# q and k transposed by the DMA crossbar instead of TensorE, in cosine attention followed by a gated feed-forward

## Chip, core and metric

One core of a Trainium2 chip. The metric is the device time of one launch in microseconds (us), the median of several executions. The engines go by short names: PE is TensorE, ACT is ScalarE, DVE is VectorE, POOL is GpSimd, SP is SyncE. Each has its own instruction stream; they meet at semaphores. PSUM is the memory that PE writes, in 8 banks.

## What is computed

Attention with q and k normalized to length 1 over 8 batches of 12 heads, 448 tokens and 64 features a head, then a multiplicative feed-forward on the 3584 tokens:

```python
q_n = q / (np.linalg.norm(q, axis=-1, keepdims=True) + 1e-06)
k_n = k / (np.linalg.norm(k, axis=-1, keepdims=True) + 1e-06)
scores = np.matmul(q_n, k_n.transpose(0, 1, 3, 2)) / tau          # tau = 0.1
scores = scores - np.max(scores, axis=-1, keepdims=True)
attn = np.exp(scores)
attn = attn / (np.sum(attn, axis=-1, keepdims=True) + 1e-09)
attn_out = np.matmul(attn, v)
x = attn_out.transpose(0, 2, 1, 3).reshape(3584, 768)
a = x @ w1                      # 768 x 1024
b = x @ w2
out = (a * b @ w3) @ w_out      # 1024 x 1024, then 1024 x 768
```

## The kernel before

The 96 heads are treated as 48 pairs of two heads; three pairs make a group that is loaded together. A pair goes through these steps:

1. q, k and v are loaded as bf16 (POOL issues the loads), with 112 tokens on the partitions and 4 tokens of each head along the row.
2. POOL squares q and k, DVE sums, ACT takes the root, and POOL scales (`prep_scale`): the result is `nrm`, bf16. A pair's q and k take 1024 columns of it on 112 partitions.
3. PE transposes each 112x128 block of `nrm` (two heads of 64 features side by side), 8 blocks a pair, into one PSUM bank, and DVE copies the bank to `qkT` in SBUF.
4. PE computes the scores of 112 keys (a chunk) against 448 queries, ACT takes exp of them, PE multiplies by v (`av`), which has a column of ones for the sum, and DVE divides (`osd`).
5. PE transposes `osd` back (`trback`), and DVE copies it to `xT`, the input of the feed-forward. The feed-forward of a batch (`a_group`, `b_group`, `out_group`) needs its six pairs. w3 @ w_out is multiplied out once.

```python
    def prep_scale(g, i, t, eng):
        if g not in nrms:
            nrms[g] = nrm_pool.tile([P, GP, 2, NJ, 2, D], BF16, tag="nrm", name="nrm")
        eng.tensor_mul(
            nrms[g][:, i, t].rearrange("p j h d -> p h j d"),
            raw_of(g, t, i),
            rns[g][:, t, 2 * i:2 * i + 2].to_broadcast([P, 2, NJ, D]))
    ...
    def tr(pp):
        g, i = divmod(pp, GP)
        n = nrms[g]
        ps = half(f"tr{pp}")
        for t in range(2):
            for j in range(NJ):
                nc.tensor.transpose(
                    ps[:, 1 - t, j * P:(j + 1) * P],
                    n[:, i, t, j].rearrange("p h d -> p (h d)"),
                    ident[:P, :P])
        qks[pp] = head_pool.tile([128, 2, S], BF16, tag="qkT", name="qkT")
        pst[pp] = ps

    def tr_copy(pp):
        nc.vector.tensor_copy(qks[pp], pst.pop(pp)[:, :, :S])

    def scores(name, chunks):
        for n, (pp, c) in enumerate(chunks):
            if c == 0:
                exps[pp] = exp_pool.tile([P, NJ, 2, S], BF16, tag="exp", name="expT")
            b = plan.bank[name][2 * n]
            sc = scs[pp, c] = ps_all[:, b:b + 2]
            for hh in range(2):
                kq = qks[pp][64 * hh:64 * hh + 64].rearrange("p t s -> p (t s)")
                nc.tensor.matmul(
                    sc[:, hh, :S], kq[:, c * P:c * P + 128], kq[:, S:],
                    start=True, stop=True)
    ...
    def av(pp, hh):
        g, i = divmod(pp, GP)
        vt = v_tiles[g % NV]
        ps = full(f"av{pp}.{hh}")[:, :NJ * (D + 1)].rearrange("p (m d) -> p m d", m=NJ)
        for m, q0 in enumerate(QT):
            for c in range(NJ):
                nc.tensor.matmul(
                    ps[:, m, :],
                    exps[pp][:, c, hh, q0:q0 + 128],
                    vt[:, 2 * i + hh, c, :D + 1],
                    start=(c == 0), stop=(c == NJ - 1))
        if hh == 0:
            osds[pp] = head_pool.tile([128, NJ, 2, D], BF16, tag="osd", name="osd")
    ...
    def mm_group(pairs, o):
        for i, (l, r) in enumerate(pairs):
            nc.tensor.matmul(o, l, r, start=(i == 0), stop=(i == len(pairs) - 1))
    ...
    def out_copy(bb, ch, cols, eng):
        ...
        elif cols.stop == DM:
            store(bb, ch, osbs.pop((bb, ch)), slice(None), (nc.sync,))
```

In the profile L291 is `prep_scale`, L310 the transposes in `tr`, L318 `tr_copy`, L328 the scores, L342 `av`, L364 and L371 the transposes back and their copy, and L377 all matmuls of the feed-forward.

The order in which each engine gets its instructions is not that of the text. A small planner (`Plan`) holds a list of steps, each with the engine or engines it may run on, an assumed duration in us, a rank, the steps it comes after and the buffers it takes and holds. It places the steps one by one, each as early as its engine, its inputs and its buffers allow; of those that could start about then, the lowest rank goes first. Attention has low ranks and the feed-forward high ones, so that feed-forward groups fill what attention leaves free. The result is one fixed order for each engine. The steps of the transposes and the scores:

```python
    plan = Plan(
        rings=dict(raw=3, vraw=2, vt=NV, sq=6, nrm=3, qkT=2, osd=2,
                   exp=3, xT=2, a_sb=KO2, big=1, out_sb=3), ...)
    ...
        add(f"sc{nb}", [("PE", 0.205 + 0.187 * len(ch))], ch[0][0] + 0.25 * ch[0][1] - 1,
            lambda e, nb=nb, ch=ch: scores(f"sc{nb}", ch),
            [f"ev{p}" for p in ps] + ([f"sc{nb - 1}"] if nb else []),
            [("exp", ("exp", p)) for p, c in ch if c == 0], [("qkT", p) for p in ps],
            banks=[tuple(slots)])
    ...
    for p in range(NP):
        g, i = divmod(p, GP)
        b, blk = divmod(p, NPAIR)
        last = p > 0
        add(f"tr{p}", [("PE", 0.4)], p - 1.2, lambda e, p=p: tr(p),
            [f"scale{p}.0", f"scale{p}.1", "ident"] + ([f"tr{p - 1}"] if last else []),
            [("qkT", ("qkT", p))], [("nrm", g)],
            slack=0.3 if g > 2 else 0.0, banks=SHORT)
        add(f"ev{p}", [("DVE", 0.54)], p - 1.1, lambda e, p=p: tr_copy(p), [f"tr{p}"],
            reads=[(f"tr{p}", None)])
```

Of the kernel before, what the change touches and what calls it, by code (L numbers as in the profile page):

```python
# [9 lines left out]
BF16 = mybir.dt.bfloat16  # L10
# [9 lines left out]
class Plan:  # L20
# [24 lines left out]
    def add(self, name, on, rank, emit, after=(), takes=(), holds=(), reads=(), kb=0, later=None,  # L45
            until=None, slack=0.0, port=False, lead=None, banks=()):
        if name in self.homes:
            on = [x for x in on if x[0] in self.homes[name]]
        self.steps[name] = dict(on=on, rank=rank, emit=emit, after=list(after), later=later,
                                takes=list(takes), kb=kb, until=until, slack=slack, port=port, lead=lead or {},  # L50
                                banks=banks)
        for user, part in reads:
            self.reads.setdefault(user, []).append((name, part))
        for key in holds:
            self.holders.setdefault(key, []).append(name)
# [45 lines left out]
    def order(self):  # L101
# [11 lines left out]
        out = []  # L113
        while ready:
# [17 lines left out]
            if st["port"] and eng in self.port:  # L132
                self.port[eng] = t + cost
            if st["kb"]:
                ring = max(ring, t + cost + self.DMA_FIRST) + st["kb"] / self.RATE
                self.end[n], self.where[n] = ring + self.DMA_LAST, "DMA"
                self.lanes.append(self.end[n])
# [17 lines left out]
def kernel(  # L155
# [28 lines left out]
    NFIRST = 6  # L184
    VROW = 80
    QT = (0, 128, 256, S - 128)

# [100 lines left out]
    def prep_scale(g, i, t, eng):  # L288
        if g not in nrms:
            nrms[g] = nrm_pool.tile([P, GP, 2, NJ, 2, D], BF16, tag="nrm", name="nrm")  # L290
        eng.tensor_mul(  # L291
            nrms[g][:, i, t].rearrange("p j h d -> p h j d"),
            raw_of(g, t, i),
            rns[g][:, t, 2 * i:2 * i + 2].to_broadcast([P, 2, NJ, D]))
# [9 lines left out]
# [4 lines that stand above are left out]
        for t in range(2):  # L308
            for j in range(NJ):
                nc.tensor.transpose(  # L310
                    ps[:, 1 - t, j * P:(j + 1) * P],
                    n[:, i, t, j].rearrange("p h d -> p (h d)"),
                    ident[:P, :P])
        qks[pp] = head_pool.tile([128, 2, S], BF16, tag="qkT", name="qkT")
        pst[pp] = ps

    def tr_copy(pp):
        nc.vector.tensor_copy(qks[pp], pst.pop(pp)[:, :, :S])  # L318
# [17 lines left out]
    def av(pp, hh):  # L336
# [10 lines left out]
        if hh == 0:  # L347
            osds[pp] = head_pool.tile([128, NJ, 2, D], BF16, tag="osd", name="osd")
        pav[pp, hh] = ps
# [8 lines left out]
    def trback(pp):  # L358
# [4 lines left out]
        for m, q0 in enumerate(QT):  # L363
            nc.tensor.transpose(  # L364
                ps[:, 0, q0:q0 + 128],
                osds[pp][:, m].rearrange("p h d -> p (h d)"), ident)
        pst["b", pp] = ps

    def tb_copy(pp):
# [82 lines left out]
    def out_copy(bb, ch, cols, eng):  # L452
# [4 lines left out]
        if at_end(bb, ch):  # L457
            store(bb, ch, osbs[bb, ch], cols, (nc.sync, nc.scalar) if cols.start else (nc.sync,))
        elif cols.stop == DM:
            store(bb, ch, osbs.pop((bb, ch)), slice(None), (nc.sync,))  # L460

# [22 lines left out]
    for eng, names in (  # L484
# [6 lines left out]
    plan = Plan(  # L491
        rings=dict(raw=3, vraw=2, vt=NV, sq=6, nrm=3, qkT=2, osd=2,
                   exp=3, xT=2, a_sb=KO2, big=1, out_sb=3),
        begin=dict(PE=1.0, ACT=3.0, DVE=1.2, POOL=1.3), homes=homes)
    add = plan.add
# [134 lines left out]
    for p in range(NP):  # L630
        g, i = divmod(p, GP)
        b, blk = divmod(p, NPAIR)
        last = p > 0
        add(f"tr{p}", [("PE", 0.4)], p - 1.2, lambda e, p=p: tr(p),
            [f"scale{p}.0", f"scale{p}.1", "ident"] + ([f"tr{p - 1}"] if last else []),
            [("qkT", ("qkT", p))], [("nrm", g)],
            slack=0.3 if g > 2 else 0.0, banks=SHORT)
        add(f"ev{p}", [("DVE", 0.54)], p - 1.1, lambda e, p=p: tr_copy(p), [f"tr{p}"],
            reads=[(f"tr{p}", None)])
        for h in range(2):  # L640
# [5 lines left out]
                lambda e, p=p, h=h: av_norm(p, h), [f"av{p}.{h}"], reads=[(f"av{p}.{h}", None)])  # L646
        add(f"tb{p}", [("PE", 0.235)], p + 1, lambda e, p=p: trback(p),
            [f"an{p}.0", f"an{p}.1"] + ([f"tb{p - 1}"] if last else []),
            [] if blk else [("xT", ("xT", b))], [("osd", p)], banks=SHORT)
        add(f"xt{p}", [("DVE", 0.31)], p - 0.2, lambda e, p=p: tb_copy(p), [f"tb{p}"],  # L650
            reads=[(f"tb{p}", None)])

# [29 lines left out]
    for b in range(B):  # L682
# [20 lines left out]
        for ch in (range(0, 3) if b % 2 == 0 else range(3, 7)):  # L703
            for cols in out_cols(bb, ch):
# [8 lines left out]
                     [("out_sb", ("out_sb", bb, ch))] if cols.start == 0 else [], [("big", bb)],  # L713
                     holds2=[("out_sb", bb, ch)] if cols.stop == DM else [],
                     lead={f"b{b}.{KO2 - 1}.c": 1.1, f"b{b}.{KO2 - 2}.c": 0.9})
    for n in range(60):
        add(f"warm{n}", [("PE", 0.78 if n < 4 else 0.39)], 10000 + n, lambda e, n=n: warm(n),
            banks=PM, later=f"warm{n - 1}" if n else None, until=6.5)
# [39 lines left out]
```

## Time and profile before

| | |
|---|---|
| time, median of 3 | 391.69 us (391.43 to 392.08) |
| span of the profiled execution | 390.0 us |
| granted PE clock | 0.999 of full speed |
| HBM read, written | 46.66 MB, 11.01 MB |
| PE transposes of q and k (L310) | 384, 212 ns each |
| DVE copies to qkT (L318) | 48, 615 ns each |
| DMAs issued by SP | 1 load and the output stores, 2.0 to 3.1 us from issue to landing |

The page gives each engine's busy time and its share of the span, then the span cut into 40 slices of 9.75 us with one digit a slice (9 is 90% busy or more), then the chain of work that ended last, followed back from the last instruction. The answers on waits list who waited for whom, with the total, the count and the longest; those on the timeline list runs of instructions with start and length. Durations of matmuls overlap, because they are pipelined: what one costs in a run is the distance from one start to the next.

### The profile page before, as it was taken

Reading aid. Unit: us, or ns where it says so; the run is one execution under the profiler, and the core shown is the slowest. Engines: PE = TensorE matmul, PEld = TensorE weight load, DVE = VectorE, ACT = ScalarE, POOL = GpSimd, SP = SyncE. Lnnn points to the kernel's source line nnn. Section 1 sums busy time; section 2 is a strip of 40 time slices with the busy share of each in tenths; the row PEclk is TensorE's granted clock in tenths of the full one; section 3 lists DMA queues with packets and bytes.
Section 4 is the critical chain, followed back from the end, with each engine's and each line's share of the span. In section 5 each row is a group of like instructions: output and inputs, shape, how many; then the busy total and the mean of one; then the engine's idle time right before and its main releaser. Section 6 shows DMA issues by size and latency. Waiting matters only on the chain.

```text
span 390.0 us, 9618 instructions
## 1 busy us (share of the span) xinstructions
PE 379.0 (97%) x3998; PEld 227.7 (58%) x3998; DVE 218.6 (56%) x500; ACT 242.0 (62%) x396; POOL 244.0 (63%) x258
## 2 busy tenths in 40 slices
PE   7789999999999999999999999999999999999995
PEld 3477666556565665556565565565656565565553
DVE  5899865587575844868477665553534444341210
ACT  5868865847756866747747776647466666652222
POOL 8687999999999989999999978361610000000000
PEclk9999999999999999999999999999999999999999
DMA  8999999637585467564738166202100121004005
GB/s 144 200 203 200 210 209 195 81 37 115 117 108 70 79 111 129 67 81 91 122 42 108 43 124 105 37 2 82 42 0 2 43 82 43 2 0 123 0 11 153
DMA packets 43707, 35.18 MB, mean 90 GB/s; under 512 B 3984, under 2 KB 37648, under 8 KB 43664
## 3 DMA queue, kind: packets, MB, share of 16 engines
q0 software_dynamic: 38384, 23.11, 43.2%
q1 hardware_dynamic: 4784, 11.07, 9.7%
q8 instruction: 31, 0.51, 0.5%
q10 hardware_dynamic: 496, 0.40, 0.3%
q14 instruction: 12, 0.10, 0.1%
HBM read 46.66 MB, written 11.01 MB: 148 GB/s over the span
## 4 chain that ended last, share of the span: by engine, by line
PE 91%; DMA 5%; DVE 2%; issue 1%; POOL 0%; DVEq 0%; POOLq 0%
PE ps L377 62%; PE ps L342 11%; PE ps L328 10%; PE ps L310 4%; DMA wo_sb<-in_moe_w_out_dram 4%; PE ps L364 3%; DMA w_sb<-in_moe_w_dram 2%; DVE nrm L291 1%; POOL raw L225 0%; DVE ss L263 0%; PE ps L390 0%; DVE qkT L318 0%; DVE osd L355 0%; DVE rn L286 0%; DVE w_sb L385 0%
## 5 line engine op out<-in xcount | busy, mean ns | idle before, releaser
L333 ACT ACTIVATE expT<-ps 112x896 bf16<-112x896 f32 x192 | 166.2, 920 | 34.1 <-PE ps L328 33.2
L377 PE MATMUL ps<-xT,w_sb 128*128 128x448 bf16 x768 | 161.3, 353 | 0.0
L377 PEld LDWEIGHTS <-w_sb 128*128 128x128 bf16 x768 | 69.2, 98 | 65.7 <-issue 12.6
L291 POOL TENSOR_TENSOR nrm<-raw,rn 112x512 bf16<-112x512 bf16 x87 | 87.9, 1037 | 11.8 <-PE ps L310 10.7
L257 POOL TENSOR_TENSOR sq<-raw 112x512 bf16<-112x512 bf16 x86 | 86.6, 1035 | 1.3 <-DMA raw<-in_k_dram 1.1
L377 PE MATMUL ps<-w_sb,abT 128*128 128x384 bf16 (+2 forms) x456 | 80.4, 323 | 0.0
L263 DVE TENSOR_REDUCE ss<-sq 112x8 f32<-112x512 bf16 x96 | 63.9, 680 | 17.9 <-POOL sq L257 16.9
L423 DVE TENSOR_TENSOR abT<-a_sb,ps 128x448 bf16<-128x448 bf16 x64 | 39.6, 619 | 56.6 <-PE ps L377 52.7
L412 ACT CAST a_sb<-ps 128x448 bf16<-128x448 f32 x64 | 34.1, 533 | 57.4 <-PE ps L377 57.4
L377 PEld LDWEIGHTS <-abT 128*128 128x128 bf16 x456 | 41.3, 98 | 30.8 <-issue 7.4
L342 PEld LDWEIGHTS <-expT 112*128 112x128 bf16 x1536 | 52.6, 97 | 7.2 <-issue 1.5
L342 PE MATMUL ps<-v_sb,expT 112*128 112x65 bf16 x1536 | 54.9, 193 | 0.8 <-POOL v_sb L242 0.8
L328 PE MATMUL ps<-qkT 64*128 64x448 bf16 x384 | 48.4, 353 | 0.4 <-DVE qkT L318 0.4
L355 DVE TENSOR_TENSOR osd<-ps,rs 128x256 bf16<-128x256 f32 x96 | 40.8, 425 | 3.3
L383 ACT COPY out_sb<-ps 128x384 f32<-128x384 f32 (+1 forms) x41 | 19.5, 476 | 36.8 <-PE ps L377 36.6
L242 POOL COPY v_sb<-vraw 112x1536 bf16<-112x1536 bf16 (+2 forms) x17 | 23.6, 1386 | 20.0 <-PE ps L342 20.0
L318 DVE COPY qkT<-ps 128x896 bf16<-128x896 bf16 x48 | 29.6, 618 | 10.9 <-PE ps L310 10.0
L371 DVE COPY xT<-ps 128x448 bf16<-128x448 bf16 x48 | 18.5, 385 | 19.6 <-PE ps L364 17.4
L328 PEld LDWEIGHTS <-qkT 64*128 64x128 bf16 x384 | 13.3, 94 | 27.6 <-issue 21.3
L310 PE MATMUL ps<-ident,nrm 112*128 112x112 bf16 x384 | 27.2, 212 | 1.3 <-DVE nrm L291 0.9
L385 DVE COPY out_sb<-ps 128x384 f32<-128x384 f32 (+1 forms) x16 | 8.6, 540 | 34.1 <-PE ps L377 34.1
L377 PE MATMUL ps<-wo_sb,w3t_sb 128*128 128x192 bf16 (+1 forms) x192 | 24.1, 273 | 2.3 <-DMA wo_sb<-in_moe_w_out_dram 2.3
(38 smaller groups left out, 208.1 us busy)
## 6 DMA issues: line engine op xcount, KB each, us to landing
vraw<-in_v_dram POOLq DMA_DIRECT2D x15, 336.0 KB, 5.8
raw<-in_q_dram POOLq DMA_DIRECT2D x15, 336.0 KB, 5.0
raw<-in_k_dram POOLq DMA_DIRECT2D x15, 336.0 KB, 6.9
w_sb<-in_moe_w_dram POOLq DMA_DIRECT2D x2, 1536.0 KB, 24.2
out_dram<-out_sb SPq DMA_DIRECT2D x7, 336.0 KB, 3.1
out_dram<-out_sb SPq DMA_DIRECT2D x8, 288.0 KB, 2.7
out_dram<-out_sb SPq DMA_DIRECT2D x8, 240.0 KB, 2.8
w_sb<-in_moe_w_dram POOLq DMA_DIRECT2D x3, 512.0 KB, 13.9
```

What stands on the lines that cost most here:

```text
L257: eng.tensor_mul(o, x, x)
L263: nc.vector.reduce_sum(sss[g][:, t, 2 * i:2 * i + 2, :], sqs.pop((g, i, t)), axis=AX.X)
L291: eng.tensor_mul(nrms[g][:, i, t].rearrange("p j h d -> p h j d"), raw_of(g, t, i), rns[g][:, t, 2 * i:2 * i + 2].to_broadcast([P, 2, NJ, D]))
L310: nc.tensor.transpose(ps[:, 1 - t, j * P:(j + 1) * P], n[:, i, t, j].rearrange("p h d -> p (h d)"), ident[:P, :P])
L318: nc.vector.tensor_copy(qks[pp], pst.pop(pp)[:, :, :S])
L328: nc.tensor.matmul(sc[:, hh, :S], kq[:, c * P:c * P + 128], kq[:, S:], start=True, stop=True)
L333: nc.scalar.activation(exps[pp][:, c], scs.pop((pp, c))[:P, :, :S], ACT.Exp, scale=1.0 / float(tau))
L342: nc.tensor.matmul(ps[:, m, :], exps[pp][:, c, hh, q0:q0 + 128], vt[:, 2 * i + hh, c, :D + 1], start=(c == 0), stop=(c == NJ - 1))
L355: nc.vector.tensor_mul(osds[pp][:, :, hh, :], ps[:, :, :D], rs.to_broadcast([128, NJ, D]))
L377: nc.tensor.matmul(o, l, r, start=(i == 0), stop=(i == len(pairs) - 1))
L412: nc.scalar.copy(a_sbs[b, fo], pms.pop(("a", b, fo))[:, :S])
L423: nc.vector.tensor_mul(abts[b // 2][:, fo, c0:c0 + S], a_sbs.pop((b, fo)), pms.pop(("b", b, fo))[:, :S])
```

## The change

From pair 6 on, `qkT` no longer comes from PE and DVE. SP issues one transposing DMA for a pair, which reads the pair's 112 x 1024 block of `nrm` in SBUF and writes all eight transposed blocks to `qkT` in SBUF. It is meant to take the transposes off PE and the copies off DVE, and to free a PSUM bank. Pairs 0 to 5 are left as they were. What goes with it:

- q and k change places inside `nrm`, so that the one transfer writes k first, as the scores want it.
- `qkT` and `osd` have three buffers in place of two.
- In the planner, the new step runs on SP with an assumed 1.3 us to issue and 2.0 us (`XBAR`) until it has landed. The output stores become steps of SP too, since they share its queue.
- A like path for the transposes back (`tb_dma`) is in the text, but is not used (`TB_DMA` is 999).

```diff
@@ -43,12 +43,12 @@
         self.where[name] = "DMA"
 
     def add(self, name, on, rank, emit, after=(), takes=(), holds=(), reads=(), kb=0, later=None,
-            until=None, slack=0.0, port=False, lead=None, banks=()):
+            until=None, slack=0.0, port=False, lead=None, banks=(), lag=0.0):
         if name in self.homes:
             on = [x for x in on if x[0] in self.homes[name]]
         self.steps[name] = dict(on=on, rank=rank, emit=emit, after=list(after), later=later,
                                 takes=list(takes), kb=kb, until=until, slack=slack, port=port, lead=lead or {},
-                                banks=banks)
+                                banks=banks, lag=lag)
         for user, part in reads:
             self.reads.setdefault(user, []).append((name, part))
         for key in holds:
@@ -131,6 +131,8 @@
             self.end[n], self.where[n] = t + cost, eng
             if st["port"] and eng in self.port:
                 self.port[eng] = t + cost
+            if st["lag"]:
+                self.end[n], self.where[n] = t + cost + st["lag"], "DMA"
             if st["kb"]:
                 ring = max(ring, t + cost + self.DMA_FIRST) + st["kb"] / self.RATE
                 self.end[n], self.where[n] = ring + self.DMA_LAST, "DMA"
@@ -183,6 +185,8 @@
     NP = B * NPAIR
     NFIRST = 6
     VROW = 80
+    TR_DMA, TB_DMA = 6, 999
+    XBAR = 2.0
     QT = (0, 128, 256, S - 128)
 
     ctx.enter_context(tc.manual_schedule())
@@ -289,7 +293,7 @@
         if g not in nrms:
             nrms[g] = nrm_pool.tile([P, GP, 2, NJ, 2, D], BF16, tag="nrm", name="nrm")
         eng.tensor_mul(
-            nrms[g][:, i, t].rearrange("p j h d -> p h j d"),
+            nrms[g][:, i, 1 - t].rearrange("p j h d -> p h j d"),
             raw_of(g, t, i),
             rns[g][:, t, 2 * i:2 * i + 2].to_broadcast([P, 2, NJ, D]))
 
@@ -308,11 +312,18 @@
         for t in range(2):
             for j in range(NJ):
                 nc.tensor.transpose(
-                    ps[:, 1 - t, j * P:(j + 1) * P],
+                    ps[:, t, j * P:(j + 1) * P],
                     n[:, i, t, j].rearrange("p h d -> p (h d)"),
                     ident[:P, :P])
-        qks[pp] = head_pool.tile([128, 2, S], BF16, tag="qkT", name="qkT")
+        qks[pp] = head_pool.tile([128, 2, S], BF16, tag="qkT", name="qkT", bufs=3)
         pst[pp] = ps
+
+    def tr_dma(pp):
+        g, i = divmod(pp, GP)
+        qks[pp] = head_pool.tile([128, 2, S], BF16, tag="qkT", name="qkT", bufs=3)
+        nc.sync.dma_start_transpose(
+            out=qks[pp].rearrange("p t (j n) -> p (t j) n", n=P),
+            in_=nrms[g][:, i].rearrange("p t j h d -> p (t j h d)"))
 
     def tr_copy(pp):
         nc.vector.tensor_copy(qks[pp], pst.pop(pp)[:, :, :S])
@@ -345,7 +356,7 @@
                     vt[:, 2 * i + hh, c, :D + 1],
                     start=(c == 0), stop=(c == NJ - 1))
         if hh == 0:
-            osds[pp] = head_pool.tile([128, NJ, 2, D], BF16, tag="osd", name="osd")
+            osds[pp] = head_pool.tile([128, NJ, 2, D], BF16, tag="osd", name="osd", bufs=3)
         pav[pp, hh] = ps
 
     def av_norm(pp, hh):
@@ -456,8 +477,6 @@
              pms.pop(("o", bb, ch, cols.start))[:, :cols.stop - cols.start])
         if at_end(bb, ch):
             store(bb, ch, osbs[bb, ch], cols, (nc.sync, nc.scalar) if cols.start else (nc.sync,))
-        elif cols.stop == DM:
-            store(bb, ch, osbs.pop((bb, ch)), slice(None), (nc.sync,))
 
     raw0 = raw_pool.tile([P, 2, 2, NJ, D], FP32, tag="raw0", name="raw0", bufs=1)
     for i, (eng, src) in enumerate(((nc.sync, q), (nc.scalar, k))):
@@ -489,9 +508,9 @@
         homes.update((name, eng.split()) for name in names.split())
     engines = {"ACT": nc.scalar, "DVE": nc.vector, "POOL": nc.gpsimd}
     plan = Plan(
-        rings=dict(raw=3, vraw=2, vt=NV, sq=6, nrm=3, qkT=2, osd=2,
+        rings=dict(raw=3, vraw=2, vt=NV, sq=6, nrm=3, qkT=3, osd=3,
                    exp=3, xT=2, a_sb=KO2, big=1, out_sb=3),
-        begin=dict(PE=1.0, ACT=3.0, DVE=1.2, POOL=1.3), homes=homes)
+        begin=dict(SP=1.5, PE=1.0, ACT=3.0, DVE=1.2, POOL=1.3), homes=homes)
     add = plan.add
 
     add("ones", [("POOL", 0.45)], -70, lambda e: ones())
@@ -631,12 +650,17 @@
         g, i = divmod(p, GP)
         b, blk = divmod(p, NPAIR)
         last = p > 0
-        add(f"tr{p}", [("PE", 0.4)], p - 1.2, lambda e, p=p: tr(p),
-            [f"scale{p}.0", f"scale{p}.1", "ident"] + ([f"tr{p - 1}"] if last else []),
-            [("qkT", ("qkT", p))], [("nrm", g)],
-            slack=0.3 if g > 2 else 0.0, banks=SHORT)
-        add(f"ev{p}", [("DVE", 0.54)], p - 1.1, lambda e, p=p: tr_copy(p), [f"tr{p}"],
-            reads=[(f"tr{p}", None)])
+        if p < TR_DMA:
+            add(f"tr{p}", [("PE", 0.4)], p - 1.2, lambda e, p=p: tr(p),
+                [f"scale{p}.0", f"scale{p}.1", "ident"] + ([f"tr{p - 1}"] if last else []),
+                [("qkT", ("qkT", p))], [("nrm", g)],
+                slack=0.3 if g > 2 else 0.0, banks=SHORT)
+            add(f"ev{p}", [("DVE", 0.54)], p - 1.1, lambda e, p=p: tr_copy(p), [f"tr{p}"],
+                reads=[(f"tr{p}", None)])
+        else:
+            add(f"ev{p}", [("SP", 1.3)], p - 1.2, lambda e, p=p: tr_dma(p),
+                [f"scale{p}.0", f"scale{p}.1", f"ev{p - 1}" if p > TR_DMA else f"tr{p - 1}"],
+                [("qkT", ("qkT", p))], [("nrm", g)], slack=0.3, lag=XBAR)
         for h in range(2):
             add(f"av{p}.{h}", [("PE", 0.49)], p + 0.5 * h, lambda e, p=p, h=h: av(p, h),
                 [f"exp{p}.{c}" for c in range(NJ)] + ["spread-" + piece_of("v", p)]
@@ -644,11 +668,16 @@
                 [] if h else [("osd", ("osd", p))], [("exp", p), ("vt", g)], banks=SHORT)
             add(f"an{p}.{h}", [("DVE", 0.62)], p + 0.5 * h - 0.5,
                 lambda e, p=p, h=h: av_norm(p, h), [f"av{p}.{h}"], reads=[(f"av{p}.{h}", None)])
-        add(f"tb{p}", [("PE", 0.235)], p + 1, lambda e, p=p: trback(p),
-            [f"an{p}.0", f"an{p}.1"] + ([f"tb{p - 1}"] if last else []),
-            [] if blk else [("xT", ("xT", b))], [("osd", p)], banks=SHORT)
-        add(f"xt{p}", [("DVE", 0.31)], p - 0.2, lambda e, p=p: tb_copy(p), [f"tb{p}"],
-            reads=[(f"tb{p}", None)])
+        if p < TB_DMA:
+            add(f"tb{p}", [("PE", 0.235)], p + 1, lambda e, p=p: trback(p),
+                [f"an{p}.0", f"an{p}.1"] + ([f"tb{p - 1}"] if last else []),
+                [] if blk else [("xT", ("xT", b))], [("osd", p)], banks=SHORT)
+            add(f"xt{p}", [("DVE", 0.31)], p - 0.2, lambda e, p=p: tb_copy(p), [f"tb{p}"],
+                reads=[(f"tb{p}", None)])
+        else:
+            add(f"xt{p}", [("SP", 0.9)], p - 0.2, lambda e, p=p: tb_dma(p),
+                [f"an{p}.0", f"an{p}.1", f"xt{p - 1}"],
+                [] if blk else [("xT", ("xT", b))], [("osd", p)], slack=0.3, lag=XBAR)
 
     line = []
     pos = {name: n for n, name in enumerate(loads)}
@@ -711,8 +740,12 @@
                      ([("ACT", 0.2 + n * 0.00065)] if n > 128 else []),
                      lambda e, bb=bb, ch=ch, cols=cols: out_copy(bb, ch, cols, e),
                      [("out_sb", ("out_sb", bb, ch))] if cols.start == 0 else [], [("big", bb)],
-                     holds2=[("out_sb", bb, ch)] if cols.stop == DM else [],
                      lead={f"b{b}.{KO2 - 1}.c": 1.1, f"b{b}.{KO2 - 2}.c": 0.9})
+                if cols.stop == DM and not at_end(bb, ch):
+                    add(f"st{bb}.{ch}", [("SP", 0.78)], 500 + b,
+                        lambda e, bb=bb, ch=ch: store(bb, ch, osbs.pop((bb, ch)), slice(None), (nc.sync,)),
+                        [line[-1] + ".c"] + [f"o{bb}.{ch}.{x.start}.c" for x in out_cols(bb, ch)],
+                        holds=[("out_sb", bb, ch)], lag=2.0)
     for n in range(60):
         add(f"warm{n}", [("PE", 0.78 if n < 4 else 0.39)], 10000 + n, lambda e, n=n: warm(n),
             banks=PM, later=f"warm{n - 1}" if n else None, until=6.5)
```

(Left out of the diff: the unused function `tb_dma`.)

More of the change, by code (lines that the diff above doesn't have):

```diff
@@ L367, in trback, with tb_dma @@
         pst["b", pp] = ps
+    def tb_dma(pp):
+        b, blk = divmod(pp, NPAIR)
+        if blk == 0:
+            xts[b] = xpool.tile([128, NPAIR, S], BF16, tag="xT", name="xT")
+        o = osds[pp].rearrange("p m h d -> p (m h d)")
+        nc.sync.dma_start_transpose(
+            out=xts[b][:, blk, :384].rearrange("p (m n) -> p m n", n=128), in_=o[:, :384])
+        nc.sync.dma_start_transpose(
+            out=xts[b][:, blk, 384:].rearrange("p (m n) -> p m n", m=1), in_=o[64:, 384:])
     def tb_copy(pp):
```

## The prediction, made before the changed kernel had run

> **What bounds the kernel now.** I read the page's busy shares and slices first, then the chain that ended last, then what TensorE (PE) waited for, then the stretches in which the part that changes stands.
>
> ```profile
> span 390.0 us, 9618 instructions
> PE 379.0 (97%) x3998; PEld 227.7 (58%) x3998; DVE 218.6 (56%) x500; ACT 242.0 (62%) x396; POOL 244.0 (63%) x258
> ...
> PE   7789999999999999999999999999999999999995
> POOL 8687999999999989999999978361610000000000
> PEclk9999999999999999999999999999999999999999
> DMA  8999999637585467564738166202100121004005
> ...
> PE 91%; DMA 5%; DVE 2%; issue 1%; POOL 0%; DVEq 0%; POOLq 0%
> ```
>
> PE is busy in every slice but the first three and the last, at the full clock, and 91% of the chain is PE. GpSimd (POOL) is just as full up to slice 23 and empty from slice 32: a possible second bound in the first 60% of the run. The DMA engines are full in slices 1 to 6 only.
>
> ```profile
> PE ps L377 <- DMA wo_sb<-in_moe_w_out_dram: 2.3, 2, 1.2
> PE ps L310 <- DVE nrm L291: 0.9, 1, 0.9
> PE ps L310 <- POOL nrm L291: 0.5, 1, 0.5
> PE ps L328 <- DVE qkT L318: 0.4, 1, 0.4
> ```
>
> These are PE's waits (total us, times, longest): all of them together come to 7 us, in the start-up. PE has an order fixed beforehand in which the feed-forward matmuls (L377) fill every gap, so the time is the sum of PE's work plus the start-up, and work taken off PE shortens the run one for one, as long as no new wait appears.
>
> **What the Trainium skill says.** "VectorE: DVE Perf Modes", section "The three transpose paths", gives 390 ns for a 128x128 bf16 transpose on TensorE, which goes to PSUM, and 1309 ns by the DMA crossbar, which goes to SBUF. The trace has 212 ns for one 112-column transpose, and below I find only 50 ns from one to the next: in a run of eight, latency isn't the cost. No run yet shows the crossbar. "DMA: Bandwidth & Descriptors", section "Latency and other measured facts", gives DMA transposes 261 GB/s in one kernel, 350 to 400 GB/s where contiguous. The same page's "Rules for kernel authors" says that DMAs of all issuing engines share the same 16 DMA engines and interleave, so the transposes share with the loads; the trace has the loads at about 200 GB/s, saturated, until 68 us. "TensorE: Matmul & The Clock Gate", "Part 4: PE-mode transpose", says that a PE transpose needs a VectorE copy after it; the trace shows that copy (L318, 615 ns).
>
> **What is removed.** The chain in a stretch in the middle (start us, length us, what), lines between left out:
>
> ```profile
> 199.99 0.40 PE ps L310 x8
> 200.39 1.14 PE ps L377 x6
> ...
> 204.94 0.67 PE ps L328 x6
> ...
> 211.27 0.97 PE ps L342 x32
> 212.24 0.40 PE ps L310 x8
> 212.64 1.14 PE ps L377 x6
> ```
>
> Eight transposes of a pair (L310) take 0.40 us of the chain, 50 ns each: the next group starts 0.40 us later, though the rows' own durations overlap. The program's instruction order has 3662 matmuls in the changed kernel against 3998: 336 = 42 pairs x 8 less. On PE: 42 x 0.40 = 16.8 us, all of it on the path, because PE is the path. On VectorE: 42 copies x 0.615 = 25.8 us, off the path (VectorE is 56% busy and mostly waits for PE); worth nothing by itself.
>
> **What is added.** 42 crossbar transposes issued by SyncE, each of 112 x 1024 bf16 = 229,376 B. Estimate from the skill's 261 GB/s: 0.88 us of transfer. Nothing measured here tells its issue and latency; the output stores, also issued by SyncE, take 2.0 to 3.1 us from issue to landing, so I choose 3 to 4 us in all (the plan in the kernel itself assumes 1.3 + 2.0). 42 x 0.88 = 37 us of DMA time lies beside other work. SyncE does nothing else but store.
>
> **Does it arrive in time?** I laid the changed order of PE instructions out with the spacings the chain shows (a 448-wide matmul 1.14/6 = 0.19 us, a score matmul 0.67/6 = 0.11, an L342 matmul 0.97/32 = 0.03). From the last score of pair p-3, which frees the third qkT buffer, to the first score of pair p lie 9 to 17, mostly 13 to 15 us; scores of successive pairs come 6.2 us apart on average. A transpose of 3 to 4 us fits both. The other condition is that nrm is ready. That is tight early on. Two rows of the timeline for pair 9, of POOL and then of PE:
>
> ```profile
> 62.06 4.04 POOL L291 TENSOR_TENSOR nrm<-raw,rn 112x512 bf16<-112x512 bf16 x4
> ...
> 65.48 0.56 PE L310 MATMUL ps<-ident,nrm 112*128 112x112 bf16 x8
> ...
> 71.91 0.74 PE L328 MATMUL ps<-qkT 64*128 64x448 bf16 x6
> ```
>
> Pair 9's q and k are scaled by 64.1 us, its scores start at 71.9: 7.8 us, and in the changed order they come about 1 us later still. For pair 6, scaled by 48.5 us, the first score moves from 51.4 to about 53.9 us: some 5.4 us for a transfer that shares full DMA engines. I count 0 to 4 us of new waits there, 1.5 in the middle. A wait on PE also lets POOL and the transposes run ahead, so it shouldn't repeat.
>
> **Sum.** 391.7 - 16.8 + 1.5 = 376.4; I say 376. As a second way, PE's instructions laid end to end with those spacings give 366.6 us before and 349.9 after: 16.7 less.
>
> **Rivals.**
> 1. The crossbar is slow: eight 112x128 blocks at the skill's 1309 ns, one after another, would be 10.5 us a pair, over the 6.2 us between pairs. The path then becomes 42 x 10.5 = 440 us of transposes after the first 50, and about 54 us of PE work after the last score: some 545 us. For it: no transpose of this size has been measured here. Against it: the 1309 ns is one small transfer, probably mostly fixed cost (my reading), and the bandwidth figure is far higher. It takes under 36 GB/s (229 KB in 6.4 us) to lose the pace. Something between, 7 to 9 us a pair, would give roughly 390 to 470.
> 2. Latency but not rate is off, 7 to 10 us from nrm to qkT (loads, stores ahead in the same queue, or SyncE waiting behind a store): PE waits at pairs 6 to 17 until it has fallen a few us behind, then no more. 379 to 384 us.
> 3. POOL becomes the bound. Its whole work is 244 us, 5.1 us a pair against PE's new 6.2, and in the second half it waited for PE and its buffers:
>
> ```profile
> POOL v_sb L242 <- PE ps L342: 20.0, 3, 9.6
> POOL nrm L291 <- PE ps L310: 10.7, 2, 7.1
> ```
>
> That is 31 us in reserve, more than the 17 taken off PE, so at most 2 or 3 us are lost: about 378.
> 4. The PE work was hidden anyway (transposes in gaps): the time would stay near 391. Against it: PE has no gaps there.
>
> **Range and chances.** About three in four for the main case or rivals 2 and 3 in their mild form (373 to 383); one in seven for a crossbar too slow for the pace, which lies far above; little near the old time. Range 371 to 386. Faster by over 2% (under 383.9): 0.77; within 2%: 0.08; slower (over 399.5): 0.15.
>
> **What would show it.** Right: the L310 group at x48 instead of x384, L318 at x6, PE busy about 362 us and still 95% or more of the span, qkT landing within 3 to 5 us of issue, PE's waits on qkT under 4 us in total and before 110 us. Wrong: score matmuls (L339 now) waiting for a DMA on qkT once per pair; a landing time over 6 us; PE's share falling below 92%; ScalarE's exp waiting for scores that wait for qkT.

## The result and the profile after

The changed kernel takes 388.34 us (387.66 to 388.86) against 391.88 us (391.43 to 392.30) for the one before: a ratio of 0.991 (95% interval 0.989 to 0.993). It is faster, but by 3.5 us, where some 15.7 had been predicted (391.7 to 376); the range of 371 to 386 missed it.

In the changed kernel's profile L324 is the transposing DMA, L314 the transposes left on PE, L329 their copy, L339 the scores, L344 exp, L353 `av`, L366 `osd`, L375 and L392 the transposes back and their copy, L398 all matmuls of the feed-forward; POOL's squares are L261 and `prep_scale` is L295. The page, the lines that answer to those shown of before:

```profile
span 385.8 us, 8994 instructions
PE 365.5 (95%) x3662; PEld 212.6 (55%) x3662; DVE 193.6 (50%) x452; ACT 244.3 (63%) x402; POOL 243.8 (63%) x258
...
PE   6989956999989999999999999999999999999995
POOL 8687993499999998999999999996210000000000
PEclk9899995999999999999999999999999999999999
DMA  9999999974999697995898859542521243004005
...
PE 74%; POOL 10%; DVE 6%; DMA 6%; issue 2%; ACT 1%; POOLq 0%; DVEq 0%
```

PE is busy for 13.5 us less, where 16.8 had been counted; part of the difference is work that ran at half clock and so took longer (below). And slices 5 and 6 are new: PE is only 5 and 6 tenths busy there, POOL 3 and 4 tenths in slices 6 and 7, and PE's clock falls to 5 tenths in slice 6. The waits of PE (total us, times, longest) name it at the top:

```profile
PE ps L339 <- DMA qkT<-nrm: 8.3, 1, 8.3
PE ps L314 <- DVE nrm L295: 2.1, 3, 0.8
```

One single wait of 8.3 us for a transposing DMA. The chain in that stretch (start us, length us, what):

```profile
45.73 2.04 POOL nrm L295 x2
47.77 0.02 issue
47.79 13.72 DMA qkT<-nrm
61.51 0.05 issue
61.55 1.30 PE ps L339 x6
62.86 4.47 PE ps L398 x16
```

Pair 6 was scaled by 47.8 us, its transpose was issued at once, and it landed 13.7 us later. The windows of 5 us (PE busy with its instruction count, then PEld, DVE, ACT and POOL, then granted clock, DMA share, GB/s) show what followed:

```profile
50.00:55.00 5.00, 3.21 (x33) 1.91 (x29) 2.81 (x7) 0.96 (x2) 5.00 (x6) 1.00 1.18 206
55.00:60.00 5.00, 0.00 (x0) 0.00 (x0) 0.00 (x0) 0.00 (x0) 4.70 (x5) 0.62 1.17 199
60.00:65.00 5.00, 3.45 (x13) 1.30 (x14) 0.00 (x0) 2.53 (x3) 1.02 (x2) 0.50 1.39 175
65.00:70.00 5.00, 5.00 (x27) 2.33 (x26) 1.15 (x2) 2.64 (x5) 0.00 (x0) 0.86 1.42 190
70.00:75.00 5.00, 5.00 (x57) 2.77 (x56) 1.12 (x4) 3.94 (x10) 2.58 (x3) 1.00 0.95 127
```

The DMA engines are full throughout. PE comes back to half its clock (0.50): the 16 feed-forward matmuls after pair 6's scores take 4.47 us of the chain, where the same 16 take 2.71 at full clock (in e4). The view of the tile qkT shows that this is no matter of every pair:

```profile
L324 SPq DMA_TRANSPOSE qkT<-nrm x42: 1222/1224/7806, 47.8 to 317.8; - x42
...
DMA to landing us min/median/max: 2.9/3.1/15.5
```

The durations on the issue line are minimum, median and maximum: the median transpose occupies SP's queue for 1.22 us and lands 3.1 us after issue. The maximum, 7.8 us, is pair 7's, issued at 49.8 us and held back already on SP.

### The profile page after: what moved, and what is told of

The parts are those of the page before. It is cut to its first block, busy times and chain, and to the rows that moved or that the text cites. A ratio compares the mean times of both kernels' runs of the same rounds, so it can differ in the third digit from the quotient of the medians. Undisturbed runs are those within 1.5% of the kernel's fastest.

```text
span 385.8 us, 8994 instructions
## 1 busy us (share of the span) xinstructions
PE 365.5 (95%) x3662; PEld 212.6 (55%) x3662; DVE 193.6 (50%) x452; ACT 244.3 (63%) x402; POOL 243.8 (63%) x258
## 3 DMA queue, kind: packets, MB, share of 16 engines
q1 hardware_dynamic: 43760, 20.71, 27.3%
## 4 chain that ended last, share of the span: by engine, by line
PE 74%; POOL 10%; DVE 6%; DMA 6%; issue 2%; ACT 1%; POOLq 0%; DVEq 0%
PE ps L398 53%; PE ps L353 9%; PE ps L339 9%; POOL sq L261 5%; POOL nrm L295 4%; DMA qkT<-nrm 4%; PE ps L375 2%; DMA wo_sb<-in_moe_w_out_dram 2%; POOL raw L229 1%; ACT expT L344 1%; DVE nrm L295 1%; DVE ss L267 1%; DVE osd L366 1%; DVE xT L392 1%; DVE w3t_sb L406 1%
## 5 line engine op out<-in xcount | busy, mean ns | idle before, releaser
L344 ACT ACTIVATE expT<-ps 112x896 bf16<-112x896 f32 x192 | 166.9, 922 | 39.5 <-PE ps L339 39.3
L398 PE MATMUL ps<-xT,w_sb 128*128 128x448 bf16 x768 | 159.8, 353 | 0.0
L398 PEld LDWEIGHTS <-w_sb 128*128 128x128 bf16 x768 | 69.4, 98 | 68.1 <-issue 13.4
L295 POOL TENSOR_TENSOR nrm<-raw,rn 112x512 bf16<-112x512 bf16 x87 | 87.8, 1036 | 11.2 <-ACT rn L284 11.1
L261 POOL TENSOR_TENSOR sq<-raw 112x512 bf16<-112x512 bf16 x86 | 86.7, 1037 | 0.2
L398 PE MATMUL ps<-w_sb,abT 128*128 128x384 bf16 (+2 forms) x456 | 80.2, 324 | 0.4 <-DVE abT L444 0.4
L398 PEld LDWEIGHTS <-abT 128*128 128x128 bf16 x456 | 41.6, 98 | 31.4 <-issue 6.7
L339 PE MATMUL ps<-qkT 64*128 64x448 bf16 x384 | 49.4, 358 | 9.4 <-DMA qkT<-nrm 8.3
L353 PEld LDWEIGHTS <-expT 112*128 112x128 bf16 x1536 | 52.6, 97 | 7.2 <-issue 1.9
L353 PE MATMUL ps<-v_sb,expT 112*128 112x65 bf16 x1536 | 54.8, 193 | 0.8 <-DVE xT L392 0.7
L404 ACT COPY out_sb<-ps 128x384 f32<-128x384 f32 (+1 forms) x45 | 21.4, 476 | 35.7 <-PE ps L398 34.7
L366 DVE TENSOR_TENSOR osd<-ps,rs 128x256 bf16<-128x256 f32 x96 | 40.7, 424 | 3.3
L392 DVE COPY xT<-ps 128x448 bf16<-128x448 bf16 x48 | 18.5, 385 | 38.2 <-PE ps L375 34.0
L339 PEld LDWEIGHTS <-qkT 64*128 64x128 bf16 x384 | 13.6, 95 | 36.4 <-issue 21.3
L365 DVE RECIPROCAL rs<-ps 128x4 f32<-128x4 f32 x96 | 16.8, 175 | 23.3 <-PE ps L353 17.6
L398 PE MATMUL ps<-wo_sb,w3t_sb 128*128 128x192 bf16 (+1 forms) x192 | 26.3, 289 | 0.8 <-DMA wo_sb<-in_moe_w_out_dram 0.8
L398 PEld LDWEIGHTS <-w3t_sb 128*128 128x128 bf16 x192 | 17.0, 102 | 8.2 <-issue 4.6
L406 DVE COPY out_sb<-ps 128x384 f32<-128x384 f32 (+1 forms) x12 | 6.4, 534 | 27.1 <-PE ps L398 24.4
## 6 DMA issues: line engine op xcount, KB each, us to landing
w_sb<-in_moe_w_dram POOLq DMA_DIRECT2D x3, 512.0 KB, 13.8
```

Of the source, the lines that this page charges most:

```text
L261: eng.tensor_mul(o, x, x)
L295: eng.tensor_mul(nrms[g][:, i, 1 - t].rearrange("p j h d -> p h j d"), raw_of(g, t, i), rns[g][:, t, 2 * i:2 * i + 2].to_broadcast([P, 2, ...
L339: nc.tensor.matmul(sc[:, hh, :S], kq[:, c * P:c * P + 128], kq[:, S:], start=True, stop=True)
L344: nc.scalar.activation(exps[pp][:, c], scs.pop((pp, c))[:P, :, :S], ACT.Exp, scale=1.0 / float(tau))
L353: nc.tensor.matmul(ps[:, m, :], exps[pp][:, c, hh, q0:q0 + 128], vt[:, 2 * i + hh, c, :D + 1], start=(c == 0), stop=(c == NJ - 1))
L366: nc.vector.tensor_mul(osds[pp][:, :, hh, :], ps[:, :, :D], rs.to_broadcast([128, NJ, D]))
```

## The experiments

Three theories at the start. A: the loads that fill the DMA engines until 68 us hold back the first transposes, PE waits once and then runs at half clock, and the rest of the change works as predicted. B: a first transpose is slow whenever it comes. C: the engines that feed PE (POOL above all, now in 10% of the chain) can't keep the new pace, and the wait is only a sign of it.

### e1: start at pair 12

```diff
-    TR_DMA, TB_DMA = 6, 999
+    TR_DMA, TB_DMA = 12, 999
```

> The crossbar starts at pair 12 in place of pair 6, at about 85 us, when the loads no longer fill the DMA engines. Theory A (the full DMA engines hold the first transposes back, 13.7 us to landing, and PE waits 8.3 us for pair 6): the wait on qkT goes to under 1 us, the granted clock to 0.99 or more, and the time is 391.9 - 36 x 0.40 = 377.5, up to 380. Rival B (the first crossbar transposes are slow whenever they come): a wait of about 8 us moves to pair 12, about 389. Rival C (POOL, near the chain after 150 us, is a bound of its own): 384 to 387 without any wait on qkT.

Measured: 381.86 us, ratio 0.973 (0.970 to 0.976). No wait on qkT is left, nor has one moved to pair 12 (the first five transposes land in 2.9 to 6.3 us), so B falls. But 4.4 us of the gain expected are missing: between 60 and 250 us PE is idle for 4.41 us, against 0.05 in the kernel before, in many small waits for DVE and ACT and one of 1.7 us. The chain leads from that one back over DVE and POOL to a load. The timeline of POOL has this line (in brackets the wait and who ended it):

```profile
240.31 4.03 POOL L261 TENSOR_TENSOR sq<-raw 112x512 bf16<-112x512 bf16 x4 [3.21 <-DMA raw<-in_k_dram]
```

That load of k took 13.9 us to land, where such loads took 6.9 before, in a stretch with transposes and output stores beside it. That these delayed it is not shown by a run of its own; e7, which has the same order here, has the same wait of 1.7 us, and e8 has not.

### e2: the planner is told of the late landing

```diff
-                [("qkT", ("qkT", p))], [("nrm", g)], slack=0.3, lag=XBAR)
+                [("qkT", ("qkT", p))], [("nrm", g)], slack=0.3, lag=12.4 if p == TR_DMA else XBAR)
```

> The transfers are those of the changed kernel; only the planner is told that pair 6 takes 12.4 us more instead of 2.0 to land, so that PE gets feed-forward groups before pair 6's scores. Theory A: the transposes still land 13 to 15 us after issue, but PE finds work meanwhile: wait on qkT under 3 us, clock 0.99, 376 to 381. Rival C: PE's wait was only one sign, POOL still loses its 11 us behind the late scores and the time stays at 384 to 388.

Measured: 384.88 us, ratio 0.981 (0.979 to 0.984). The first three transposes landed 12.3 to 16.3 us after issue, and PE, which now had feed-forward groups to do, didn't wait for any of them. Yet the time is 4 us above the most that theory A expected, and inside C's range. PE's timeline 30 us later says why:

```profile
95.31 0.74 PE L339 MATMUL ps<-qkT 64*128 64x448 bf16 x6 [0.79 <-DVE osd L366]
96.68 0.38 PE L375 MATMUL ps<-ident,osd 128*128 128x128 bf16 x4 [0.63 <-ACT expT L344]
98.84 1.30 PE L339 MATMUL ps<-qkT 64*128 64x448 bf16 x6 [1.78 <-DVE xT L392]
100.40 1.92 PE L353 MATMUL ps<-v_sb,expT 112*128 112x65 bf16 x32 [0.26 <-ACT expT L344]
```

The feed-forward work that filled the gap was gone when the pairs from 10 on, postponed, came one right behind the other: between 89.9 and 107.3 us PE has no feed-forward matmul at all, waits for the engines of attention, 4 us between 90 and 100 us, and the clock falls again (0.57 between 100 and 110 us; the matmuls of 100.40 take 1.92 us instead of 1.14). Work to hide a wait behind was borrowed from the next stage and missing there. Behind those waits stands POOL: the chain runs over its squares and scalings from 85.9 to 101.8 us. So where PE has nothing but attention to do, C's mechanism does cost time.

### e3: no transposes at all from pair 6 on

```diff
     def tr_dma(pp):
-        g, i = divmod(pp, GP)
-        qks[pp] = head_pool.tile([128, 2, S], BF16, tag="qkT", name="qkT", bufs=3)
-        nc.sync.dma_start_transpose(...)
+        qks[pp] = qks[5]
```

This leaves out the transposes of 42 pairs; the order of the rest is that of the changed kernel.

> Leaves the transposes from pair 6 on out altogether: the scores of all later pairs read pair 5's qkT; the order of all other instructions is that of the changed kernel. Theory A: this is what the prediction counted without its new waits, 391.9 - 16.8 = 375, at most 377; the difference to the changed kernel, 11 to 13 us, is the whole price of late transfers. Rival C: 382 or more, because the other engines can't feed PE at the new pace even with no transfer to wait for (though nrm buffers come free sooner here).

Measured: 377.45 us, ratio 0.962 (0.960 to 0.965). Half a us above the most that A expected, this is the ceiling of the change in this order: 10.9 us below the changed kernel. The 10.9 are nearly the 8.35 us of wait plus 2.3 us of slow matmuls right after it (16 matmuls in 4.54 instead of 2.77 us and the scores in 1.30 instead of 0.74, by the timelines under e4). C falls as the cause of the changed kernel's loss: with no transfer to wait for, the other engines feed PE almost well enough; 2.3 us of small waits between 60 and 250 us are left.

### e4: less load in the way

```diff
-            em = lambda e, a=weights[name]: load_w(*a)
+            em = (lambda e, a=weights[name]: load_w(*a)) if name != "w20" else None
-        mm_group([(w2_sb[...], xts[b][:, ko, :])
+        mm_group([(w1_sb[...], xts[b][:, ko, :])
```

This leaves the load of w2 out and computes with w1 in its place.

> Leaves the load of w2 out (w1 is used in its place), so that 3 MB less are read between 33 and 60 us; the order is that of the changed kernel. Theory A: the DMA engines run dry earlier, pair 6's transpose lands 5 to 10 us after issue instead of 13.7, PE's wait falls to 0 to 5 us and the time to 377 to 384. Rival B (a first transpose is slow whatever else runs): 13 to 14 us and a wait of 8 us as before, 387 to 388.

Measured: 382.70 us, ratio 0.977 (0.974 to 0.980). Pair 6's transpose lands 9.2 us after issue instead of 13.7 and PE's wait is 3.77 us instead of 8.35. That is A again, with the load as the lever: nothing about the transposes or their order was touched. But the DMA engines did not run dry, as had been expected. From 52 to 54 us the queue of the loads still moved 488 packets, 0.24 MB, beside 486 of the transposes; in the changed kernel, from 52 to 58 us, 536 packets, 1.10 MB, beside 535. The loads that are left go in packets of 0.5 KB, those of w2 in packets of 2 KB, and the transposes' packets got through 2.7 times as fast; e7 and e8 show why. PE's timeline, first of this run, then of the changed kernel:

```profile
56.07 0.74 PE L339 MATMUL ps<-qkT 64*128 64x448 bf16 x6 [3.77 <-DMA qkT<-nrm]
56.74 2.77 PE L398 MATMUL ps<-wo_sb,w3t_sb 128*128 128x384 bf16 x16
```

```profile
61.55 1.30 PE L339 MATMUL ps<-qkT 64*128 64x448 bf16 x6 [8.35 <-DMA qkT<-nrm]
62.79 4.54 PE L398 MATMUL ps<-wo_sb,w3t_sb 128*128 128x384 bf16 x16
```

After a wait of 3.77 us the same work runs at full speed; after 8.35 us it takes 1.6 to 1.8 times as long. (The trace is of an execution of 379.82 us with a mean clock of 1.000; the four others, at 0.980 to 0.996, took 382.01 to 383.80, so the median holds some 3 us that this trace doesn't show.)

### e5: start at pair 9

```diff
-    TR_DMA, TB_DMA = 6, 999
+    TR_DMA, TB_DMA = 9, 999
```

> The crossbar starts at pair 9, scaled at about 64 us, when the loads fill the DMA engines for some 4 us more. Theory A: the first transpose lands 6 to 12 us after issue, PE waits 0 to 4 us for it, and the time lies between that of the start at pair 12 and that at pair 6: 380 to 385. If it is only the number of transposes taken off PE that counts, it should be 1.2 us below the start at pair 12, 380.7 or less.

Measured: 377.59 us, ratio 0.963 (0.961 to 0.964). Better than expected (380 to 385), and faster than both kernels: the ceiling of e3 is reached, although three pairs fewer are taken off PE. Its first transpose is issued at 63.5 us and lands 8.4 us later, at 71.9; pair 9's scores start at 73.7. The transpose is late here too, by the measure of the others, but nobody needs it sooner. The view of the first two transposes, and the line of PE:

```profile
L324 SPq DMA_TRANSPOSE qkT<-nrm x2: 1314/1664/2015, 63.5 to 65.5; - x2
...
DMA to landing us min/median/max: 8.4/8.6/8.7
```

```profile
73.73 0.74 PE L339 MATMUL ps<-qkT 64*128 64x448 bf16 x6
```

PE is idle for 1.6 us between 60 and 250 us. But 39% of the chain is POOL now (10% in the changed kernel), so work taken off PE beyond this would soon meet POOL; no run tests it. And e1, which doesn't wait for a transpose either, is 4.3 us slower with only three pairs fewer on the crossbar: part of e5's success is an order that happens to fit.

### e6: the planner assumes 5 us to landing (start at pair 12)

```diff
-    XBAR = 2.0
+    XBAR = 5.0
```

> Start at pair 12, and the planner assumes 5.0 us to landing in place of 2.0, nearer to the 5 to 8 us that transposes beside loads took. If the 4.4 us of PE waits after 60 us that are left with the start at pair 12 come from an order that is too tight for the landing times, they fall to about 2 and the time to 379 to 380. If they come from loads that the transposes delay (POOL waiting for raw), nothing changes: 381 to 383.

Measured: 380.24 us, ratio 0.969 (0.968 to 0.971), 1.6 us below e1, with 3.0 us of idle PE between 60 and 250 us instead of 4.4. Taken alone it looks as if e1's order had been too tight; e12 below contradicts.

### e7 and e8: what is held back, the crossbar or small pieces?

```diff
+    def probe(pp):                       # pairs 6 and 7; start of the crossbar at pair 12
+        nc.sync.dma_start(out=probe_sb[pp][:, :, :128],
+                          in_=nrms[g][:, i].rearrange("p t j h d -> p (t j) (h d)"))
```

The spare tile's rows are 128 elements long in e7, so that a partition's 2 KB are one piece, and 136 in e8, so that they are eight pieces of 256 bytes.

> Start at pair 12, and besides, SP copies the nrm block of pairs 6 and 7 (112 x 1024 bf16, 2 KB from each partition) to a spare tile by plain DMAs, at about 48 and 50 us, where the changed kernel had its first transposes. Nobody waits for the copies. If full DMA engines hold back whatever SP issues, they land 10 us or more after issue. If it is the transpose with its 256-byte pieces that suffers, they land in 3 to 5 us.

> As the run before, with the same bytes cut into 896 pieces of 256 bytes, the number of pieces that the transpose has. If the number of pieces decides, they land about 13 us after issue, like the transpose, whatever the plain copies of 2 KB pieces took; if the crossbar itself is at fault, they land as those did.

Measured, from the views of the copying line in e7 and in e8 (durations on SP's queue, start, and the time from issue to landing):

```profile
L332 SPq DMA_DIRECT2D probe_sb<-nrm x2: 526/580/635, 47.6 to 49.6; - x2
...
DMA to landing us min/median/max: 6.3/6.3/6.4
```

```profile
L332 SPq DMA_DIRECT2D probe_sb<-nrm x2: 607/696/784, 47.4 to 49.4; - x2
...
DMA to landing us min/median/max: 13.8/14.7/15.6
```

The same 229,376 bytes, at nearly the same moment, from the same queue: 6.3 us in big pieces (between the two forecasts), 14.7 us in pieces of 256 bytes, and the transpose took 13.7. So it isn't the crossbar: a plain copy in 256-byte pieces waits as long while the loads run. (One execution each: 382.16 and 380.27 us; the copies are on no path.) The Trainium skill, "DMA: Bandwidth & Descriptors", section "SWDGE vs HWDGE vs iDMA", says that each DMA engine goes round its queues in turn and changes over at packet boundaries. The trace has it so here. The DMA queues between 53 and 55 us (packets, MB, the time of the packets as a share of 16 engines), e7 first, then e8; q0 is the queue of the loads, q1 that of SP:

```profile
q0 software_dynamic: 138, 0.28, 74.2%
q1 hardware_dynamic: 136, 0.25, 37.1%
```

```profile
q0 software_dynamic: 177, 0.36, 95.1%
q1 hardware_dynamic: 180, 0.05, 17.4%
```

One packet of SP goes for each packet of a load, whatever their sizes, so SP gets 0.25 MB in these 2 us with its big packets and 0.05 MB with its small ones. The changed kernel's transposes show the same (535 packets for 536, under e4). The latency adds up from this: in e8 the first copy's first packet starts 4.2 us after issue, its 912 packets take 8.3 us, while the loads move 908, and 1.3 us later it has landed, 13.8 in all; in e7 it is 4.0, 1.9 for 128 packets and 0.4, 6.3 in all. The first 4 us are the same for both and for the transpose of pair 6; in quiet, at the transpose of 74.5 us in the changed kernel, they are 1.2. Why they are longer beside loads stays open. The same page's "Why small descriptors are slow (HBM only)" says that SBUF to SBUF transfers are spared the penalty of small descriptors that it describes, a cost to their bandwidth; what small pieces cost here, a factor of 2.3 in latency, is their place beside full load queues.

### e9: no crossbar, only the side changes

```diff
-    TR_DMA, TB_DMA = 6, 999
+    TR_DMA, TB_DMA = 999, 999
```

> No pair goes by the crossbar; the third buffers of qkT and osd and the stores as planned steps of SP stay. If these side changes cost or bring something of their own, the time is off 391.9 by over 1 us. Theory A: it isn't, 391 to 392.5.

Measured: 394.91 us, ratio 1.007 (1.006 to 1.009): the side changes cost 3.0 us, where none had been expected. (Its profiled execution took 1351.51 us, unlike the others at 394.54 to 394.94; its trace is not used, and without it the median is 394.89.) With two buffers for qkT again, and two or three for osd, the planner's order is that of the kernel before on every engine, stores included. So it is qkT's third buffer, which lets the planner set transposes earlier, and the order that follows from it. Where in the run the 3.0 us are lost isn't shown.

### e10: pairs 6 to 8 alone by the crossbar

```diff
-        if p < TR_DMA:
+        if not TR_DMA <= p < 9:
```

> Pairs 6, 7 and 8 alone go by the crossbar, all others by PE. Theory A: the loss is made here and nowhere else, 8 us of wait and some 2.5 us of half-clock matmuls after it, with only 3 x 0.40 us off PE: 391.9 - 1.2 + 10.9 = about 401, and slower than before. Rival (part of the loss is spread over the later transposes): 395 to 398.

Measured: 404.61 us, ratio 1.032 (1.031 to 1.034). PE's wait:

```profile
PE ps L339 <- DMA qkT<-nrm: 8.5, 1, 8.5
```

From e9: 394.9 - 3 x 0.40 = 393.7; 404.6 is 10.9 above it, the sum that parts the changed kernel from e3. The some 3 us over the expected 401 are those of e9, which the expectation had not counted. The loss is made by the first transposes.

### e11: start at pair 8

```diff
-    TR_DMA, TB_DMA = 6, 999
+    TR_DMA, TB_DMA = 8, 999
```

> The crossbar starts at pair 8, which is scaled at about 52.5 us and whose scores come at about 59 in PE's order: 6 to 7 us for a transfer that takes 11 to 14 us with the loads still running. Theory A: PE waits 4 to 7 us for it, with a lower clock after it: 382 to 386, 5 us or more above the start at pair 9, though one pair more is taken off PE. If lateness doesn't set the loss, it is 377.2.

Measured: 382.23 us, ratio 0.976 (0.974 to 0.977), 4.6 us above e5 for one pair earlier. The transpose, issued at 51.7 us, lands after 11.1, and PE's timeline shows the wait and the clock after it:

```profile
62.85 0.55 PE L339 MATMUL ps<-qkT 64*128 64x448 bf16 x2 [4.25 <-DMA qkT<-nrm]
63.34 4.66 PE L398 MATMUL ps<-xT,w_sb 128*128 128x448 bf16 x12
```

Twelve such matmuls take 2.4 us at full clock.

### e12: start at pair 9, the planner assumes 5 us

```diff
-    TR_DMA, TB_DMA = 6, 999
-    XBAR = 2.0
+    TR_DMA, TB_DMA = 9, 999
+    XBAR = 5.0
```

> Start at pair 9 with 5.0 us to landing in the planner. At pair 12 this brought 1.6 us; the start at pair 9 has only 2 us of PE waits left after 60 us, so 376 to 378 against 377.6.

Measured: 381.25 us, ratio 0.973 (0.971 to 0.975): a miss, 3.7 us above e5. No wait on qkT in either, but 4.4 us of idle PE between 60 and 250 us instead of 1.6. What brought 1.6 us at pair 12 costs 3.7 here. So the assumed landing time works through the whole order that the planner happens to make, and is no rule.

## Why the prediction was wrong, step by step

The measured parts in one sum: 391.9, + 3.0 for the order with the third qkT buffer (e9), - 17.5 for transposes that leave PE (e9 to e3), + 10.9 for the late first transposes (e3 to the changed kernel) = 388.3. Each term is the difference of two runs, so they add up by construction; that an order costs the same 3.0 us with and without the crossbar is not shown. Without e9, the way from the kernel before to e3 is 14.4 us of the 16.8 counted, and the 2.3 us of small waits of PE in e3 are nearly the rest.

- **What bounds the kernel**: right. PE is the path, and what leaves PE shortens the run nearly one for one: 14.4 us (kernel before to e3) or 17.5 (e9 to e3) for 16.8 predicted. DVE lost 25.0 us of work (25.8 predicted); no run tests what that is worth by itself.
- **What is added**: "I choose 3 to 4 us in all" is right for the median (3.1 us) and was taken from output stores in quiet stretches. The DMA time was mis-sized: the share of SP's queue went from 9.7% of 390.0 us to 27.3% of 385.8, which is 67.5 us or 1.6 us for each transpose, where the prediction estimated 0.88.
- **Does it arrive in time? The step that failed.** "Some 5.4 us for a transfer that shares full DMA engines. I count 0 to 4 us of new waits there, 1.5 in the middle." The place was right (pair 6, the DMA engines full) and the margin about right, but the transfer took 13.7 us and the wait was 8.35. The prediction saw that the DMA engines are shared, but not how: they go packet for packet (e7, e8), so the transpose's 928 packets had to wait for about as many packets of the loads, most of them eight times as large, after 4 us to the first packet.
- **What wasn't counted at all**: PE's clock after the wait, 2.3 us; and an order that fits less well, to which the third buffer of qkT belongs: 3.0 us in e9, 2.3 us of small waits in e3.
- **"It shouldn't repeat"**: right, the wait came once (e10). Of the marks set beforehand, the median landing, the x48 transposes left on PE and PE's 95% of the span held; the wait of under 4 us on qkT and PE's 362 us did not (365.5; 362.9 in e3), and a landing of over 6 us, a sign of being wrong, came at the first transposes.
- **Rivals**: rival 2 had the mechanism, latency and not rate, and pairs 6 to 17, but with 7 to 10 us to landing. Rival 1, a crossbar too slow for the pace, was given one chance in seven: wrong by far, 2.9 us in quiet. Rival 3: POOL did lose 11.1 us, waiting for ACT's root behind the late scores of pair 6, and entered the chain, but e3 and e10 leave next to nothing for it to cost in this kernel; in e2 it did cost. Rival 4, "near 391", came nearest in number and has no part in it: e3 shows that the work was not hidden.
- **Two slips that nothing rests on**: by its own sum, 7 to 9 us a pair give some 400 to 480 us, not 390 to 470; and POOL is empty from slice 30 on, counted from 0 as for the DMA engines, not 32.

What stays open: how much of the 2 to 4 us of small waits on DVE and ACT in e1, e6 and e12 belongs to loads delayed by transposes, and how much to the order as such. e1 shows one such load; no run here parts the two.

## What to carry to other kernels

Before work is moved from a busy engine to the DMA engines, look at the slices in which they are full, and ask in what pieces the new transfer goes and in what pieces the traffic beside it: its latency in the quiet part of the run says nothing about that stretch. Then start the new path where the time between its input and its first reader exceeds the latency measured there: here at pair 9, 377.6 us, instead of at pair 6, 388.3. That removes the wait, and no more: starts at pair 12 meet the rule as well and take 380.2 and 381.9, so the order has to be measured. And price everything that changes a planned order, a spare buffer too.

## What the runs showed of the hardware that wasn't expected

- 229,376 bytes from SBUF to SBUF beside full load queues landed in 6.3 us as pieces of 2 KB and in 14.7 us as pieces of 256 bytes; a crossbar transpose of the same bytes took 13.7, and 2.9 us in quiet.
- A transpose can be held back already while SyncE issues it: 7.8 us instead of 1.22 for the second one.
- While both had work, the queues of the loads and of SP took turns one packet for one: 177 to 180 in e8, 138 to 136 in e7 (53 to 55 us), with packets of 2 KB on one side and of 256 bytes or 2 KB on the other.
- PE's clock after a wait: still 1.00 after 3.77 us (e4), about half after 4.25 us (e11) and 8.35 us. It isn't the length of one wait alone: in e2 it fell where the longest wait was 1.78 us, with PE busy for 6.0 of the 10 us from 90 to 100. And in e11 it fell well inside the wait of 58.6 to 62.85 us: its mean is 1.00 from 56 to 60 us and 0.63 from 60 to 64, which with only the two clocks that these traces have, full and half, puts the fall near 61 us. Few cases, so no rule.
